# Reading a matmul's moving operand as two interleaved halves, in a fused attention and two feed-forward layers on one core

## The chip, the core and the metric

The kernel runs on one core of a Trainium2 chip. A core has a matrix engine (TensorE, PE in the rows below, with PEld for its weight loads), a vector engine (VectorE, DVE), a scalar engine (ScalarE, ACT), GpSimd (POOL) and a sync engine (SP) that issues most transfers. The metric is the device time of one execution in microseconds (us); lower is better. All arithmetic on the device counts, and the arrangement of inputs and outputs on the host doesn't.

A matmul on TensorE takes two operands from the on-chip memory SBUF. The stationary one (`lhsT`) is loaded first, as weights. The moving one (`rhs`) is then streamed through, column by column, and each of its columns gives one column of the result in the accumulation memory, PSUM.

## The reference

```
def _attn_ref(q, k, v, tau):                       # each 1 x 6016 x 256
    qn = q / (np.linalg.norm(q, axis=1, keepdims=True) + 1e-06)
    kn = k / (np.linalg.norm(k, axis=1, keepdims=True) + 1e-06)
    s = kn.transpose(0, 2, 1) @ qn / tau           # 256 x 256
    a = np.exp(s - s.max(-1, keepdims=True))
    a /= a.sum(-1, keepdims=True) + 1e-09
    return v @ a
x = attn.reshape(6016, 256)
h = x @ moe_w_in;  x = (h * np.clip(h + 3, 0, 6) / 6) @ moe_w_out     # 256 -> 2048 -> 256
h = x @ moe2_w_in; r = np.maximum(h, 0); out = (r * r) @ moe2_w_out   # 256 -> 2048 -> 256
```

All arrays are 32-bit floats; the weights of both layers arrive as 64-bit floats and are brought to 32 bits on the chip.

## The kernel before, in words

**Attention.** The 256 x 256 scores are summed over 47 tiles of 128 tokens (`score`, line 315), in plain float32. The softmax is applied to them, and the result `et` is multiplied into the first layer's input weights `wi1` (`m1_first`, `m1_whole`; tiles `mp`), so that the first layer can work on the tokens of `v` directly.

**The two layers.** The 6016 tokens are taken in 6 passes of two blocks each, of 512 columns (5 passes) or 448 columns (the last): `WIDTHS = [512] * 5 + [448]`. So there are 12 pairs of layer and pass, (j, p). Everything is laid out with features on the partitions and tokens in the columns, so that the tokens are always the moving operand. The only products whose moving operand isn't tokens are the 48 of tile `mp`, where it is a row of 512 columns of `wi1`. Each 32-bit operand is split into a high and a low part of type float32r (`split`), and a product of two such operands is three matmuls, high by high, low by high, high by low. `passes` (lines 332 to 339) issues these three in a row, and `low_last` (line 318 on) issues the same three with the low weight parts last.

From the second pair on, a layer's input product goes by a Strassen scheme (`strassen`): for each of 8 units of 256 hidden features, seven products (tiles `y`, `q`, `x`) take the place of eight. The output products (`group`, tile `acc`) are added up in four PSUM banks over the whole pass. The first pair (0, 0) has its own code: `first_products` (line 685), `whole_product` through `low_last` (line 327), and `second_both` (line 734).

Between an input product and its output product ScalarE and VectorE copy, add, gate and split the tile (`copy_out`, `add`, `relu`, `act`, `hi`, `lo`); line 132 is the subtraction that gives a low part. The order of all this is a list of events, each put at a place in a row of slots (`at`, `extra`, `run`), and every engine works through its own instructions in that order.

**What is streamed.** Each moving operand of these products is a stretch of one tile row, of 512 or 448 neighbouring columns. The result of a layer's last product goes through `evict` to `x2_d` in main memory (or to `out`), and is read back as the next layer's input. On the host, `kernel` lays out the tokens in `vt`, and the last lines put `out` back into the order of the reference.

Of the kernel before, what the change touches and what calls it, by code (L numbers as in the profile page):

```python
# [16 lines left out]
P = 128  # L17
C = 256
NTOK = 6016
DFF = 2048  # L20
NT = NTOK // P
KC = C // P
# [40 lines left out]
def attention_then_two_ffns(  # L63
# [44 lines left out]
    def bank(shape, name, tag=None):  # L108

        if tag is None:  # L110
            tag = "yxyq"[turn[0] % 4]
            turn[0] += 1
        return ps_h.tile(shape, F32, tag=tag, name=name, bufs=2 if tag == "y" else 1)
# [9 lines left out]

    def f32(x):
        return x.bitcast(F32)

    def split(hi, lo, x, part=2, eng=nc.vector):

        if part != 1:
            nc.scalar.copy(hi, x)  # L130
        if part != 0:
            eng.tensor_tensor(out=lo, in0=x, in1=f32(hi), op=ALU.subtract)  # L132
# [48 lines left out]
    wi1, wo1 = {}, {}  # L181
# [44 lines left out]
    def second_in(u):  # L226
# [25 lines left out]
        def rests(i):  # L252
            a, w = ((slice(0, S1), x[:, :S1, :]), (slice(S1, None), st))[i]
            nc.vector.tensor_tensor(out=lo[:, a, :], in0=w, in1=f32(hi[:, a, :]), op=ALU.subtract)

        def keep_out():
            for t, d in zip((hi, lo), wa2_d[u // 2]):
                nc.sync.dma_start(out=d[:, u % 2, :, :], in_=f32(t))
# [60 lines left out]
    def low_last(ps, pairs, weights=True, only=2):  # L319

        n = len(pairs)
        parts = ((0, 0), (0, 1)), ((1, 0),)
        for part in parts if only == 2 else parts[only:only + 1]:
            for i, (a, b) in enumerate(pairs):
                for x, y in part:
                    w, v = (a[x], b[y]) if weights else (b[y], a[x])
                    nc.tensor.matmul(  # L327
                        ps, lhsT=w, rhs=v, start=i == 0 and (x, y) == (0, 0), stop=i == n - 1 and x == 1
                    )

    def passes(ps, pairs, start=True, stop=True, more=False):


        n = len(pairs)
        for i, ((ah, al), (bh, bl)) in enumerate(pairs):
            first, last = start and i == 0, stop and i == n - 1
            nc.tensor.matmul(ps, lhsT=ah, rhs=bh, start=first, stop=False, skip_group_check=more)  # L337
            nc.tensor.matmul(ps, lhsT=al, rhs=bh, start=False, stop=False, skip_group_check=more)  # L338
            nc.tensor.matmul(ps, lhsT=ah, rhs=bl, start=False, stop=last, skip_group_check=more)  # L339

    with tc.manual_schedule():
# [9 lines left out]
        t = 0  # L351

        for gi, n in enumerate(GROUPS):
# [13 lines left out]
            for j in range(n):  # L367
                x = src[:, j * 2 * C:(j + 1) * 2 * C]
# [67 lines left out]
        x0 = {}  # L436
# [79 lines left out]
        def m1_first(i, part):  # L516
            if part != 1:
                mps[0, i] = bank([P, 512], f"mp0_{i}")
            low_last(mps[0, i], [
                ([t[:, i, j * P:(j + 1) * P] for t in et], [t[:, j, :] for t in wi1[0]]) for j in range(KC)  # L520
            ], only=part)

        def m1_whole(c4, i):
            mps[c4, i] = bank([P, 512], f"mp{c4}_{i}")
            low_last(mps[c4, i], [
                ([t[:, j, :] for t in wi1[c4]], [t[:, i, j * P:(j + 1) * P] for t in et]) for j in range(KC)
            ], False)
# [48 lines left out]
        def m1_sum(c4, i):  # L576

            if i == 0:
                m1_st[c4] = beside(max(c4, 1), 0).rearrange("p (u a c) -> p u a c", u=2, a=4)
            m = [m32[c4][:, k, :].rearrange("p (u f c) -> p u f c", u=2, f=2) for k in range(KC)]  # L580
            combine(i, m1_st[c4], [[t[:, :, f, :] for f in range(2)] for t in m], lambda t, i: t[:, :, i, :], idle_first(c4 < 2))

        def m1_sums_split(c4, u, part):
            hi, lo = (t[:, u, S1:, :] for t in wa1[c4])
            split(hi, lo, m1_st[c4][:, u, :, :], part, idle_first(c4 < 2))
# [30 lines left out]
        acc = {}  # L616
# [5 lines left out]
        def group(j, p, u, f, n, d, gs, first, last):  # L622

            w = WIDTHS[p]
            if first:
                acc[j, p, n, d] = ps_acc.tile([P, WMAX], F32, tag="acc", name=f"acc{j}_{p}_{n}_{d}")[:, :w]
            wo = wo_parts(j, u)
            at = f * C + d * P
            passes(acc[j, p, n, d], [([wo[:, i, at:at + P] for i in range(2)], gs)], first, last)
# [36 lines left out]
        hs = {}  # L666
# [3 lines left out]
        def weight0(f, k):  # L670
            c4, u, odd = f // 4, f // 2 % 2, f % 2
            if odd and k == 0:
                return [a21[c4][:, i, u, :] for i in range(2)]
            return [t[:, u, (A12, A22)[odd] if k else A11, :] for t in wa1[c4]]

        def first_products():
            for at in range(2):
                n, f = steps[at]
                hs[at] = bank([P, WMAX], f"h0_{n}_{f}")[:, :w0]
            for k in range(KC):  # L680
                for part in ((0, 0), (0, 1)), ((1, 0),):
                    for at in range(2):
                        n, f = steps[at]
                        for a, b in part:
                            nc.tensor.matmul(
                                hs[at], lhsT=weight0(f, k)[a], rhs=x0[k, n][b],
                                start=k == 0 and (a, b) == (0, 0), stop=k == KC - 1 and a == 1,
                            )

        def whole_product(at):  # L690
            if at < len(steps):
                n, f = steps[at]
                name = f"h0_{n}_{f}"
                if at in (2, 3):
                    hs[at] = ps_acc.tile([P, WMAX], F32, tag="acc", name=name)[:, :w0]
                else:
                    hs[at] = bank([P, WMAX], name)[:, :w0]
                low_last(hs[at], [(weight0(f, k), x0[k, n]) for k in range(KC)])
# [27 lines left out]
        def second_both(n, f, gs):  # L726
            u, at = f // 2, f % 2 * C
            if f == 0:
                for d in range(KC):
                    acc[0, 0, n, d] = ps_acc.tile([P, WMAX], F32, tag="acc", name=f"acc0_0_{n}_{d}")[:, :w0]  # L730
            for part in ((0, 0), (1, 0)), ((0, 1),):
                for d in range(KC):
                    for i, k in part:
                        nc.tensor.matmul(  # L734
                            acc[0, 0, n, d], lhsT=wo1[u][:, i, at + d * P:at + (d + 1) * P], rhs=gs[k],
                            start=f == 0 and (i, k) == (0, 0), stop=f == KF - 1 and k == 1,
                        )

        def drain(limit):
            while len(pending) > limit:  # L740
                second_both(*pending.pop(0))
# [24 lines left out]
        def extra(place, go):  # L766


            while any(abs(place - x) < (APART if place > 0 else APART_FIRST) for x in taken):
                place += 0.3  # L770
            taken.append(place)
            at(place, go)
            return place
# [61 lines left out]
        def strassen(j, p, u, at0):  # L835
# [7 lines left out]
            def mult(r):  # L843
                wa = wa1[c4] if j == 0 else wa2[c4]
                if r == B11:
                    s["y"] = bank([P, WMAX], f"y{name}", "y")[:, :w]
                elif r == B21:
                    s["x"] = bank([P, WMAX], f"x{name}", "x")[:, :w]
                elif r == T3:
                    s["q"] = bank([P, WMAX], f"q{name}", "q")[:, :w]  # L850
                to = {B21: "x", T3: "q", T4: "q"}.get(r, "y")
                passes(
                    s[to], [([t[:, ui, WEIGHT[r], :] for t in wa], operands[j, p, r])],
                    r in (B11, B21, T3), more=r not in (B11, B21, T3),
                )
# [66 lines left out]
        k = 0  # L922
# [11 lines left out]
        for c4, x in ((0, -100), (1, -72), (2, 10), (3, 34)):  # L934
            for i in range(4):
                x = extra(x, lambda c4=c4, i=i: m1_sum(c4, i)) + 1
            for u in range(2):
                at(x + 2 + u, lambda c4=c4, u=u: m1_sums_split(c4, u, 0))
            for u in range(2):
                x = extra(x + 4 - 3 * u, lambda c4=c4, u=u: m1_sums_split(c4, u, 1))  # L940
# [49 lines left out]
        def four_steps():  # L990
# [44 lines left out]
            run(-(len(steps) - 4) * SLOTS / 4)  # L1035

        first_products()
        relu0(0)
        four_steps()
        for a, (n, f) in enumerate(steps):  # L1040
            if a < 4:
                continue
            part, since = divmod(a + M1_LEAD, 8)
# [36 lines left out]
        for x, go in zip(LEFT_AT, [(n, f, d, gs) for n, f, gs in pending for d in range(KC)], strict=True):  # L1080
            n, f, d, gs = go
# [48 lines left out]
```

## Time and profile before

| | |
|---|---|
| Time of one execution, median of 3 runs | 1036.01 us (1035.68 to 1036.33) |
| Span of the profiled execution, first to last instruction | 1033.6 us |
| Left of the median outside that span | 2.4 us |
| TensorE busy | 1027.0 us, 99% of the span |
| TensorE weight loads busy | 866.0 us, 84% |
| VectorE busy | 849.0 us, 82% |
| ScalarE busy | 664.8 us, 64% |
| GpSimd busy | 42.6 us, 4% |

The profile is of one execution, for which the span is given and no time of its own besides; the median stands 2.4 us above it. Busy time is the union of an engine's instructions. A matmul's record is longer than the time until the next one starts, because matmuls overlap in the engine; the pace of TensorE is therefore read from the start times of its matmuls, not from their durations.

### The profile page before, as it was taken

The numbers are of one execution on the slowest core, as the hardware profiler recorded it, in microseconds if no ns is written. First come the engines' busy times: TensorE is split into PE (matmuls) and PEld (weight loads), VectorE is DVE, ScalarE is ACT, GpSimd is POOL, SyncE is SP. The second block draws the span as 40 slices with busy tenths as digits, with TensorE's granted clock in tenths as the row PEclk, the third lists the DMA queues.
The fourth block names the chain that finished last, engine by engine and source line by source line (L and its number), as shares of the span: only waits on it lengthen the run. The fifth ranks groups of instructions, "written<-read, shape, count | busy, mean of one in ns | idle before, by whom it ended". The sixth has DMA issues, their size and how long they took to land.

```text
span 1033.6 us, 12918 instructions
## 1 busy us (share of the span) xinstructions
PE 1027.0 (99%) x4618; PEld 866.0 (84%) x4618; DVE 849.0 (82%) x1419; ACT 664.8 (64%) x1202; POOL 42.6 (4%) x42
## 2 busy tenths in 40 slices
PE   9999999999999999999999999999999999999998
PEld 8888888888888888888998888888888888888997
DVE  5899988889989989889988688688778688778765
ACT  7788877778787778878775445455445455445543
POOL 2212330000000000000000000000000000000000
PEclk9999999999999999999999999999999999999999
DMA  9811212003403403403745002002002000100100
GB/s 360 345 58 42 81 47 96 1 1 139 137 1 123 152 1 118 153 1 131 263 160 185 1 1 82 0 1 82 1 1 75 7 1 25 52 1 1 41 1 36
DMA packets 26368, 77.64 MB, mean 75 GB/s; under 512 B 2880, under 2 KB 5056, under 8 KB 26304
## 3 DMA queue, kind: packets, MB, share of 16 engines
q1 hardware_dynamic: 26160, 76.70, 20.9%
q8 instruction: 36, 0.59, 0.2%
q14 instruction: 28, 0.23, 0.1%
q10 hardware_dynamic: 144, 0.11, 0.0%
HBM read 52.95 MB, written 23.86 MB: 74 GB/s over the span
## 4 chain that ended last, share of the span: by engine, by line
PE 99%; DVE 0%; ACT 0%; issue 0%; POOL 0%; POOLq 0%
PE acc L339 15%; PE acc L338 15%; PE acc L337 15%; PE y L338 8%; PE y L337 8%; PE y L339 8%; PE s L315 4%; PE h L327 4%; PE acc L734 4%; PE q L337 4%; PE q L339 4%; PE q L338 4%; PE x L339 2%; PE x L337 2%; PE x L338 2%; PE mp L327 1%
## 5 line engine op out<-in xcount | busy, mean ns | idle before, releaser
L132 DVE TENSOR_TENSOR gs<-g,gs 128x512 fp32r<-128x512 f32 (+1 forms) x384 | 263.5, 687 | 58.8 <-ACT gs L886 48.2
L339 PE MATMUL acc<-gs,wo 128*128 128x512 f32 (+1 forms) x708 | 272.6, 385 | 0.1
L338 PE MATMUL acc<-gs,wo 128*128 128x512 f32 (+1 forms) x708 | 272.5, 385 | 0.0
L337 PE MATMUL acc<-gs,wo 128*128 128x512 f32 (+1 forms) x708 | 272.4, 385 | 0.0
L886 ACT CAST gs<-g 128x512 fp32r<-128x512 f32 (+1 forms) x352 | 208.0, 612 | 27.8 <-DVE g L877 19.0
L339 PEld LDWEIGHTS acc<-gs,wo 128*128 128x128 f32 x708 | 132.9, 188 | 25.3 <-DVE gs L132 0.5
L338 PEld LDWEIGHTS acc<-gs,wo 128*128 128x128 f32 x708 | 132.9, 188 | 24.3
L337 PEld LDWEIGHTS acc<-gs,wo 128*128 128x128 f32 x708 | 132.9, 188 | 24.3
L859 ACT COPY se<-y 128x512 f32<-128x512 f32 (+1 forms) x88 | 50.7, 576 | 123.4 <-PE y L339 123.3
L863 DVE TENSOR_TENSOR h<-q,se 128x512 f32<-128x512 f32 (+1 forms) x88 | 59.6, 677 | 64.9 <-ACT se L859 64.4
L859 ACT COPY su<-y 128x512 f32<-128x512 f32 (+1 forms) x88 | 50.8, 577 | 87.1 <-PE y L339 76.2
L882 DVE SCALAR_TENSOR_TENSOR g<-h 128x512 f32<-128x512 f32 (+1 forms) x144 | 97.0, 674 | 0.0
L869 ACT ACTIVATE r<-h,three 128x512 f32<-128x512 f32 (+1 forms) x120 | 85.5, 713 | 8.0 <-DVE h L863 7.7
L877 DVE SCALAR_TENSOR_TENSOR g<-r,h 128x512 f32<-128x512 f32 (+1 forms) x120 | 80.8, 673 | 3.9 <-ACT r L869 3.8
L871 ACT ACTIVATE r<-y 128x512 f32<-128x512 f32 (+1 forms) x48 | 28.3, 589 | 62.8 <-PE y L339 62.8
L863 DVE TENSOR_TENSOR h<-q,su 128x512 f32<-128x512 f32 (+1 forms) x88 | 59.5, 676 | 1.5
L863 DVE TENSOR_TENSOR h<-x,sa 128x512 f32<-128x512 f32 (+1 forms) x88 | 59.2, 673 | 0.0
L859 ACT COPY sa<-y 128x512 f32<-128x512 f32 (+1 forms) x88 | 50.7, 576 | 7.3 <-PE y L339 1.3
L882 DVE SCALAR_TENSOR_TENSOR g<-y,r 128x512 f32<-128x512 f32 (+1 forms) x48 | 32.7, 681 | 23.6 <-ACT r L871 23.0
L734 PE MATMUL acc<-gs,wo 128*128 128x512 f32 x180 | 45.0, 389 | 0.0
L315 PE MATMUL s<-qk 128*128 128x256 f32 x188 | 42.1, 385 | 0.0
L315 PEld LDWEIGHTS s<-qk 128*128 128x128 f32 x188 | 36.1, 194 | 5.1 <-DMA qk<-in_qk 0.2
(245 smaller groups left out, 1803.3 us busy)
## 6 DMA issues: line engine op xcount, KB each, us to landing
qk<-in_qk SPq DMA_DIRECT2D x21, 512.0 KB, 10.0
wo<-in_w_out SPq DMA_DIRECT2D x16, 512.0 KB, 5.6
wi<-in_w_in SPq DMA_DIRECT2D x10, 512.0 KB, 5.5
x2d<-o SPq DMA_DIRECT2D x20, 256.0 KB, 2.5
raw<-x2d SPq DMA_DIRECT2D x10, 512.0 KB, 5.5
out<-o SPq DMA_DIRECT2D x20, 256.0 KB, 2.3
raw<-in_vt SPq DMA_DIRECT2D x8, 512.0 KB, 5.8
wo2d<-wo2s SPq DMA_DIRECT2D x8, 512.0 KB, 2.9
```

Source lines behind the costliest of these rows:

```text
L132: eng.tensor_tensor(out=lo, in0=x, in1=f32(hi), op=ALU.subtract)
L315: nc.tensor.matmul(s_ps[i], lhsT=x[:, C + i * P:C + (i + 1) * P], rhs=x[:, :C], start=(t == 0), stop=(t == NT - 1))
L337: nc.tensor.matmul(ps, lhsT=ah, rhs=bh, start=first, stop=False, skip_group_check=more)
L338: nc.tensor.matmul(ps, lhsT=al, rhs=bh, start=False, stop=False, skip_group_check=more)
L339: nc.tensor.matmul(ps, lhsT=ah, rhs=bl, start=False, stop=last, skip_group_check=more)
L734: nc.tensor.matmul(acc[0, 0, n, d], lhsT=wo1[u][:, i, at + d * P:at + (d + 1) * P], rhs=gs[k], start=f == 0 and (i, k) == (0, 0), stop=f = ...
L859: nc.scalar.copy(s[tag], s["y"])
L863: nc.vector.tensor_tensor(out=s[which], in0=s[ps], in1=s[tag], op=ALU.add)
L869: nc.scalar.activation(s["r" + which], h, AF.Relu, bias=three)
L877: nc.vector.scalar_tensor_tensor(out=g, in0=s["r" + which], scalar=6.0, in1=h, op0=ALU.min, op1=ALU.mult)
L882: nc.vector.scalar_tensor_tensor(out=g, in0=h, scalar=0.0, in1=r, op0=ALU.max, op1=ALU.mult)
L886: nc.scalar.copy(gs[which][0], s["g" + which])
```

## The change

A new helper `halves` views a row of w columns as w/2 pairs: the first column of the first half, the first of the second half, the second of the first half, and so on. In the layers' matmuls the moving operand is now this view. The tile in SBUF is the same, and so are its place and its size; only the order in which its columns are streamed differs. Neighbours in that order lie 256 columns apart (224 in the last pass), which is 1024 or 896 bytes of each partition's row, and column c of the result holds another token than before.

Four such products follow on each other for every token (into and out of each layer), so the tokens come out permuted four times over. The last lines of `kernel` compute that permutation and undo it on the host. Where the moving operand is a row of `wi1`, the columns of the weights are laid out on the host so that the product comes out in the old order (`interleaved`). The score product and the small ones of the softmax keep their plain rows.

```
+    def halves(x):
+
+        return x.rearrange("p (a b) -> p b a", a=2)
...
# low_last
-                        ps, lhsT=w, rhs=v, start=i == 0 and (x, y) == (0, 0), stop=i == n - 1 and x == 1
+                        ps, lhsT=w, rhs=halves(v), start=i == 0 and (x, y) == (0, 0), stop=i == n - 1 and x == 1
...
# passes
             first, last = start and i == 0, stop and i == n - 1
+            bh, bl = halves(bh), halves(bl)
             nc.tensor.matmul(ps, lhsT=ah, rhs=bh, start=first, stop=False, skip_group_check=more)
...
# first_products
-                                hs[at], lhsT=weight0(f, k)[a], rhs=x0[k, n][b],
+                                hs[at], lhsT=weight0(f, k)[a], rhs=halves(x0[k, n][b]),
...
# second_both
-                            acc[0, 0, n, d], lhsT=wo1[u][:, i, at + d * P:at + (d + 1) * P], rhs=gs[k],
+                            acc[0, 0, n, d], lhsT=wo1[u][:, i, at + d * P:at + (d + 1) * P], rhs=halves(gs[k]),
...
# kernel, on the host
+    def interleaved(w):
+        return w.reshape(KC * P, DFF // 512, 256, 2).transpose(0, 1, 3, 2).reshape(KC * P, DFF)
...
-        "w_in1": w_in(inputs["moe_w_in"]),
+        "w_in1": w_in(interleaved(inputs["moe_w_in"])),
...
-        res[t:t + 2 * w] = got[p, :, :, :, :w].transpose(2, 3, 1, 0).reshape(2 * w, KC, P)
+        at = np.arange(w)
+        for _ in range(4):
+            at = at.reshape(2, w // 2).T.reshape(w)
+        part = np.empty((P, KC, 2, w), got.dtype)
+        part[..., at] = got[p, :, :, :, :w]
+        res[t:t + 2 * w] = part.transpose(2, 3, 1, 0).reshape(2 * w, KC, P)
```

Every engine has the same instructions in the same order in both kernels; only an operand of each of these matmuls reads otherwise.

## Rows read from the trace of the kernel before

**Rows 1.** The page's chain of work that ended last, by engine.
```profile
PE 99%; DVE 0%; ACT 0%; issue 0%; POOL 0%; POOLq 0%
```
**Rows 2.** Waits of PE: who waited for whom, us in total, times, longest.
```profile
PE busy L294 <- POOL both L119: 1.1, 1, 1.1
PE mp L327 <- ACT eth L502: 0.5, 1, 0.5
```
**Rows 3.** Windows: stretch, PE, PEld, DVE, ACT, POOL busy (instructions), granted clock, DMA.
```profile
0.00:49.00 49.00, 47.41 (x225) 41.74 (x225) 34.23 (x64) 37.04 (x68) 13.18 (x19) 1.00 0.94 370
49.00:1028.80 979.80, 979.60 (x4394) 824.23 (x4394) 814.39 (x1355) 627.48 (x1134) 29.38 (x23) 1.00 0.17 60
1028.80:1033.60 4.80, 0.00 (x0) 0.00 (x0) 0.39 (x1) 0.30 (x1) 0.00 (x0) 0.99 0.52 191
```
**Rows 4.** Windows over the whole span, PE of one line alone: L337, L734, L327, L685.
```profile
0.00:1033.60 1033.60, 509.37 (x1324) 1.00 0.21 75
```
```profile
0.00:1033.60 1033.60, 45.02 (x180) 1.00 0.21 75
```
```profile
0.00:1033.60 1033.60, 56.76 (x228) 1.00 0.21 75
```
```profile
0.00:1033.60 1033.60, 2.88 (x12) 1.00 0.21 75
```
**Rows 5.** Groups of L338 with 448 columns, shapes kept apart, one for each tile.
```profile
L338 PE MATMUL acc<-gs,wo 128*128 128x448 f32 x128 | 46.8, 366 | 0.0
...
L338 PE MATMUL y<-x,wa_0l 128*128 128x448 f32 x16 | 5.9, 368 | 0.0
...
L338 PE MATMUL q<-x,wa_0l 128*128 128x448 f32 x8 | 2.9, 364 | 0.0
...
L338 PE MATMUL x<-x,wa_0l 128*128 128x448 f32 x4 | 1.4, 362 | 0.0
```
**Rows 6.** Timeline of PE, 600 to 606 us: start, us, what. First and last of 28.
```profile
599.70 0.39 PE L338 MATMUL acc<-gs,wo 128*128 128x512 f32 x1
599.93 0.39 PE L339 MATMUL acc<-gs,wo 128*128 128x512 f32 x1
...
605.82 0.39 PE L338 MATMUL y<-x,wa_3l 128*128 128x512 f32 x1
```
**Rows 7.** Timeline of PE, 968 to 972 us. First and last of 21.
```profile
967.77 0.36 PE L339 MATMUL y<-x,wa_0h 128*128 128x448 f32 x1
967.97 0.36 PE L337 MATMUL y<-x,wa_1h 128*128 128x448 f32 x1
...
971.82 0.36 PE L338 MATMUL acc<-gs,wo 128*128 128x448 f32 x1
```
**Rows 8.** Timeline of PE, 25 to 43 us, like instructions merged: start, us, what.
```profile
24.66 17.00 PE L315 MATMUL s<-qk 128*128 128x256 f32 x78
41.49 1.73 PE L409 MATMUL nrm<-both,scratch 128*128 128x1 f32 x15
```
**Rows 9.** Instructions of L315 and L409: duration ns min/median/max, first and last start.
```profile
L315 PE MATMUL s<-qk x188: 379/379/634, 4.3 to 47.9; 128*128 128x256 f32 x188
```
```profile
L409 PE MATMUL nrm<-both,scratch x16: 167/250/250, 41.5 to 43.1; 128*128 128x1 f32 x16
```
**Rows 10.** Windows as in 3, of the stretch with the densest work beside PE.
```profile
160.00:600.00 440.00, 440.00 (x1980) 371.32 (x1979) 385.27 (x664) 327.72 (x589) 0.00 (x0) 1.00 0.27 94
```

## The prediction

> **What bounds the kernel now.** I read the chain of waits first. TensorE holds 99% of the chain that ended last [rows 1], and its own list of waits is two entries long, 1.6 us together [rows 2]. So nothing feeds TensorE late; the time is the number of its matmuls times their pace. The window table then says where the changed matmuls lie: all in the 979.8 us from 49.0 to 1028.8 us, in which TensorE is busy for 979.6 us at a granted clock of 1.00, which is the 2.4 GHz level [rows 3]. Ahead of it lies the score stage, and behind it 4.8 us of eviction and output; neither is touched.
>
> The counts come from the lines. Line 337 issues 1324 matmuls, and 338 and 339, the other two of the same three, as many; 734 issues 180, 327 issues 228 and 685 issues 12 [rows 4]. That is 3 x 1324 + 420 = 4392. Those with 448 columns are, for each of lines 337 to 339, 128 for `acc`, 16 for each of four groups of `y`, 8 for each of four of `q`, 4 for each of four of `x` [rows 5]: 128 + 4 x 28 = 240, so 720 in all. The other 3672 have 512 columns.
>
> The pace comes from start times. In the timeline of a steady stretch 27 starts lie between 599.70 and 605.82 us: 226.7 ns for a matmul of 512 columns [rows 6]. With 448 columns 20 of them take from 967.77 to 971.82 us: 202.5 ns [rows 7]. The check: 3672 x 0.2267 + 720 x 0.2025 = 832.4 + 145.8 = 978.2 us of the 979.6 in the window.
>
> **What one column costs.** At 2.4 GHz 512 columns at one per clock would be 213.3 ns, and 448 would be 186.7. The layers' matmuls are 13.4 and 15.8 ns above that. The score product, plain float32, shows another pace: 78 matmuls of 256 columns take 17.00 us, the last of them 0.38 [rows 8, 9], so each takes (17.00 - 0.38) / 77 = 215.8 ns, two clocks per column and only 2.5 ns over. And 15 matmuls of one column each, whose pace is that of loading 128 columns of weights, take (1.73 - 0.25) / 14 = 106 ns [rows 8, 9], 0.83 ns per weight column.
>
> Side by side: wherever else this trace shows TensorE taking 4-byte elements from SBUF, it takes one per 0.83 to 0.84 ns (score stream, weights). Only the layers' plain rows come at one per 0.443 ns, nearly two per such beat, and they alone miss the clock by 6%. I read this as a supply of columns that runs at its limit, and that gets there because two neighbours arrive together. That is an argument, not a row; the score product also has two clocks of arithmetic per column, so its pace may be the array's and not the memory's.
>
> **The change, part by part.** No instruction is added, removed or moved, on any engine or queue, and no wait. The transfers have the same sizes and shapes. The host's new orders cost nothing on the chip. Evictions, gates and splits work on plain rows as before. What is left is one thing: 4392 matmuls stream their 512 or 448 columns so that each column lies 1024 or 896 bytes from the one before. Nothing hides a change of pace there, since TensorE has no idle time to give; each ns per matmul is 4392 x 1 ns = 4.4 us.
>
> The trace has no moving operand read in such an order, so I bound its price. From below: the best pace that a row shows for 512 clocks of streaming is the score product's 215.8 ns [rows 8], a gain of 10.9 ns, and 188.8 ns for 448 columns, a gain of 13.7. From above: if no two columns come together any more, each costs what one costs alone. By the score stream that is 0.843 ns per column, 431.6 ns for 512 and 377.7 for 448. If instead the pace of today is halved outright, it is 453.4 and 405.0 ns.
>
> I take the upper end, at the score product's price. The plain rows already miss the clock at 0.443 ns per column, so the supply has no slack in which a worse order could hide, and the new order takes away the one thing that sets these reads apart from the two slower kinds: that what is wanted next lies beside what was just read.
>
> The sum: 3672 x (431.6 - 226.7) ns = 752.4 us, and 720 x (377.7 - 202.5) = 126.1 us, together +878.5. From the profiled span: 1033.6 + 878.5 = 1912.1, and with the 2.4 us by which the median stands above the span, **1914.5 us**. At exactly one column per 1.2 GHz beat (426.7 and 373.3 ns) it is +857 and 1893 us; at double today's pace +978 and 2014 us. VectorE's 849 us and ScalarE's 665 us of work [rows 3] don't grow and fall under half of the span, so neither can become the bound.
>
> [...]
>
> **The rivals.**
>
> *Faster: the 10.9 ns go away.* The place is the stream of each layers' matmul. That two kinds of matmul stream for 512 clocks, one 2.5 ns over the clock and the other 13.4, shows that the excess isn't the engine's own cost for a matmul. If it comes from reading along a row (always drawing on the part of the memory that is already busy), alternating between two places could spare it. Price: 3672 x 10.9 + 720 x 13.7 ns = 40.0 + 9.9 = 49.9 us, 986 us. It decides from 0.5 ns per matmul on (2.1 us, 0.2%). Against it: the excess is there in every tile and buffer alike, and nothing says that distance helps rather than hurts. Beside TensorE, VectorE has 385.3 us of work in 440 [rows 10]; shortened by 5% that stretch would be 419 us, which still holds it, though some of the gain could become waits.
>
> *No change: the order doesn't matter.* If the column supply fetches element by element and its limit is in the count of bytes, any order costs 226.7 ns. The time stays 1036 us. For it: the stream's addresses are known ahead. Against it: the two slower kinds of read above. [...]
>
> *Slower, but far from double.* The excess is paid per jump in address order and merely grows. Doubled, it is 3672 x 13.4 + 720 x 15.8 ns = 60.6 us, 1097 us; between there and 1893 any multiple is possible. For it: an excess exists that a mere break could enlarge. Against it: it needs a supply that mostly manages single columns at 0.44 ns, of which no row speaks.
>
> **How the numbers follow.** I give the full price, one column at a time, 0.40; the smaller slowdown 0.12; no change 0.14; the gain 0.34, rather high for what the rows support, because the excess of 13.4 ns is real and the order of reading is one of the few things that could be behind it. Differences under 0.2% (2 us) can't be told from no change by such runs, so: faster 0.34, same 0.14, slower 0.52. The likeliest case is 1914 us, with a range of its own of 1890 to 2016. To hold the time 8 times in 10 the range has to take in both the gain and the full price, since leaving out either leaves out more than 2 in 10: 984 to 2016 us. It is wide because the one price that decides isn't in the trace and multiplies 4392 times.
>
> **What would show it right or wrong.** In the timeline of the changed kernel the starts of 512-column matmuls in a steady stretch should lie 427 to 454 ns apart, those of 448 columns 373 to 405, alike in `acc`, `y`, `q`, `x`; the score product should keep 215.8 ns. TensorE should stay at 99% of the chain and at a granted clock of 1.00, and VectorE should show long idle times that TensorE ends. If the starts lie 216 ns apart, the supply is helped by distance; if they lie at 226.7, the order is free; and if TensorE shows waits, something else moved that I have not seen.

## The result, and the profile after

The changed kernel takes 996.39 us (median of 4 runs, 996.07 to 996.87) against 1036.17 us before: ratio 0.9615, 95% interval 0.9601 to 0.9629. It is faster by 39.8 us, where 1914 us was forecast.

The page of the kernel after, its head and the first lines of its chain that ended last:

```profile
span 995.1 us, 12918 instructions
...
PE 983.1 (99%) x4618; PEld 869.0 (87%) x4618; DVE 845.0 (85%) x1419; ACT 676.5 (68%) x1202; POOL 42.0 (4%) x42
...
PE 84%; DVE 7%; ACT 4%; DMA 2%; issue 2%; SPq 1%; ACTq 0%; DVEq 0%
```

The same instructions, and TensorE is still busy for 99%. But the chain, 99% TensorE before [rows 1], now goes through VectorE and ScalarE for 11%. The pace is in the timeline of TensorE, 600 to 606 us, first and last of 30 rows (start, us, what), and 935 to 939 us, first and last of 23:

```profile
599.69 0.38 PE L343 MATMUL q<-x,wa_3l 128*128 128x512 f32 x1
599.91 0.38 PE L344 MATMUL q<-x,wa_3h 128*128 128x512 f32 x1
...
605.95 0.38 PE L342 MATMUL x<-x,wa_0h 128*128 128x512 f32 x1
```

```profile
934.71 0.35 PE L344 MATMUL x<-x,wa_1h 128*128 128x448 f32 x1
934.90 0.35 PE L342 MATMUL acc<-gs,wo 128*128 128x448 f32 x1
...
938.88 0.35 PE L342 MATMUL y<-x,wa_1h 128*128 128x448 f32 x1
```

29 starts in 6.26 us are 215.9 ns for 512 columns (226.7 in [rows 6]), and 22 in 4.17 us are 189.5 ns for 448 (202.5 in [rows 7]). Over the whole trace nearly every start-to-start time is 215 or 216 and 189 or 190 ns, in all tiles alike, 215.8 and 189.2 on the mean without the waits. These two differ by 26.6 ns for 64 columns, which gives an estimate of 0.416 ns a column. That is 2.4 GHz if a column takes one clock, the frequency that the prediction counts with; [rows 3] show a granted clock of 1.00 and no frequency. 512 and 448 such clocks are 213.3 and 186.7 ns, and both paces lie 2.5 ns above them. The excess of the plain rows, 13.4 and 15.8 ns, is down to that. The windows show what the pace did not give (columns as in [rows 3]):

```profile
49.00:990.00 941.00, 935.34 (x4394) 827.33 (x4394) 811.49 (x1358) 638.93 (x1134) 28.84 (x23) 1.00 0.18 62
```

At the new pace 4392 matmuls are 3672 x 0.2158 + 720 x 0.1892 = 928.6 us; the stretch is 941.0. Some 12 us of it are waits and what follows them, against under 2 before. TensorE's list of waits, two entries long before [rows 2], reads now, in part:

```profile
PE acc L739 <- DVE gs L136: 1.5, 2, 0.8
...
PE h L331 <- DVE g L716: 1.0, 2, 0.5
PE acc L344 <- DVE gs L136: 0.7, 3, 0.3
PE acc L739 <- DVE wo L136: 0.6, 1, 0.6
PE h L331 <- DVE wa_1l L557: 0.6, 1, 0.6
```

One of them in the timeline, 72 to 76.5 us:

```profile
75.13 0.48 PE L331 MATMUL h<-x,wa_1l 128*128 128x512 f32 x1
76.17 0.48 PE L331 MATMUL h<-x,wa_1l 128*128 128x512 f32 x1 [0.57 <-DVE wa_1l L557]
76.49 0.38 PE L331 MATMUL h<-x,wa_1h 128*128 128x512 f32 x1
```

The start at 76.17 comes 1.04 us after the last one instead of 0.22, and the next one needs 0.32 us: the list's 0.57 us is a loss of 0.93. Added up from the start times, between 50 and 150 us 7.5 us are lost in this way, and later 4.2.

### The profile page after: what moved, and what is told of

Same layout as the page of the kernel before. It is cut to its first block, busy times and chain, and to the rows that moved or that the text cites. A ratio compares the mean times of both kernels' runs of the same rounds, so it can differ in the third digit from the quotient of the medians.

```text
span 995.1 us, 12918 instructions
## 1 busy us (share of the span) xinstructions
PE 983.1 (99%) x4618; PEld 869.0 (87%) x4618; DVE 845.0 (85%) x1419; ACT 676.5 (68%) x1202; POOL 42.0 (4%) x42
## 4 chain that ended last, share of the span: by engine, by line
PE 84%; DVE 7%; ACT 4%; DMA 2%; issue 2%; SPq 1%; ACTq 0%; DVEq 0%
PE acc L344 14%; PE acc L342 14%; PE acc L343 14%; PE y L342 7%; PE y L344 7%; PE y L343 7%; PE q L342 4%; PE q L344 4%; PE q L343 4%; PE s L319 4%; DVE gs L136 2%; PE x L342 2%; PE x L344 2%; PE x L343 2%; ACT gs L134 1%
## 5 line engine op out<-in xcount | busy, mean ns | idle before, releaser
L344 PE MATMUL acc<-gs,wo 128*128 128x512 f32 (+1 forms) x708 | 265.9, 376 | 0.8 <-DVE gs L136 0.7
L342 PE MATMUL acc<-gs,wo 128*128 128x512 f32 (+1 forms) x708 | 264.9, 374 | 0.0
L343 PE MATMUL acc<-gs,wo 128*128 128x512 f32 (+1 forms) x708 | 264.9, 374 | 0.0
L344 PEld LDWEIGHTS acc<-gs,wo 128*128 128x128 f32 x708 | 133.8, 189 | 19.5 <-DVE gs L136 3.6
L343 PEld LDWEIGHTS acc<-gs,wo 128*128 128x128 f32 x708 | 133.8, 189 | 15.5
L342 PEld LDWEIGHTS acc<-gs,wo 128*128 128x128 f32 x708 | 133.8, 189 | 15.5
L739 PEld LDWEIGHTS acc<-gs,wo 128*128 128x128 f32 x180 | 33.5, 189 | 8.6 <-DVE gs L136 2.6
```

The lines of the kernel that those rows point to most:

```text
L739: nc.tensor.matmul(acc[0, 0, n, d], lhsT=wo1[u][:, i, at + d * P:at + (d + 1) * P], rhs=halves(gs[k]), start=f == 0 and (i, k) == (0, 0), ...
```

## The experiments

**1. Form, number of streams, and the weight load.** Three theories were on the table for the excess of the plain row: it is paid where stream and weight load meet (meeting), it is the stream's own and distance spares it (row), or the operand's form counts (form).

```
plain_pairs   halves(x) = x.rearrange("p (b a) -> p b a", a=2)
quarters      halves(x) = x.rearrange("p (a b) -> p b a", a=4)
w2_plain      kernel before; lhsT=wo[:, i, f * C + d:(f + 1) * C:2]      # acc, was at:at + P
w2_halves     kernel after;  the same
```

> The layers' moving operand is viewed as pairs of neighbours, (0, 1), (2, 3), and so on: the three-dimensional form of the change with the order of before. Three theories for the excess of 10.9 ns per 512-column matmul. Meeting: the stream (one column per clock) runs through the rows twice as fast as the next weight load (one per two clocks), and the excess is paid where they meet; two halves run at the weights' speed and never meet them. Row: the excess belongs to the stream alone, which is too fast for one place, and is spared by alternating between distant ones. Form: an operand with two free dimensions starts sooner, whatever the order. Meeting and row expect 226.7 ns and about 1036 us here, form 215.8 ns and about 996 us.

> Four interleaved quarters in place of two halves (the host's orders follow). Row and form expect what halves gave, 215.8 ns and about 996 us, since neighbours in the order are still far apart. Meeting expects part of the excess back: each place is now passed through at half the weights' speed, so the load overtakes the stream, half as often as the stream overtook the load before; some 5 ns of the 10.9, about 221 ns and 1015 us.

> The kernel before, with its plain rows, but the output products (tile acc, 2304 of the 4392 matmuls) load every second column of 256 as weights in place of 128 neighbours, so that the load runs through the row as fast as the stream does (the host orders the output weights to match). Meeting expects 215.8 ns in acc and still 226.7 ns in y, q and x, about 1010 us. Row and form expect 226.7 ns everywhere and about 1036 us, since the stream is unchanged.

> The changed kernel with the same weights at every second column in the output products. Meeting expects the excess back in acc, where the load now runs twice as fast as the interleaved stream: some 5 to 11 ns, about 1010 to 1022 us. Row and form expect 215.8 ns everywhere and about 996 us.

Measured, one execution each: `plain_pairs` 1036.07 us at 226.7 ns, but its trace shows an operand with one dimension of 512, so the form was merged away and the run tells nothing of it. That form alone gains nothing shows in `near8` below, whose operand keeps three dimensions (2, 2, 128) and stays at 226.7 ns. `quarters` 1249.5 us, slower by a fifth, which no theory had expected. `w2_plain` 1051.6 us: acc rose to 233.2 ns instead of falling. `w2_halves` 996.5 us: 215.8 ns as with neighbouring weights. The meeting theory fell on both sides, and the row and form theories by the quarters, where both had expected 215.8 ns. Timeline of `quarters`, 700 to 706 us, first and last of 22 rows (21 starts in 5.95 us, 283 ns; 278 on the mean of the whole trace):

```profile
699.81 0.45 PE L343 MATMUL y<-x,wa_2l 128*128 128x512 f32 x1
...
705.76 0.45 PE L343 MATMUL x<-x,wa_2l 128*128 128x512 f32 x1
```

**2. Distance and step.** The host's orders follow each view of the moving operand, in these runs and in those that come after, so that the tokens come out in place.

```
near512    x.rearrange("p (c a b) -> p c b a", c=2, a=2)
near16     x.rearrange("p (c a b) -> p c b a", a=2, b=4)
even_odd   x.rearrange("p (a b) -> p b a", b=2)
step4      x.rearrange("p (a b) -> p b a", b=4)
```

> Two interleaved streams as in the change, but half as far apart: each half of the row is itself read as two interleaved quarters, 512 bytes apart (448 in the last pass). Quarters gave 278 ns, so either the distance of 512 bytes is bad or four streams are too many. Two theories. Count: the column supply keeps two places of a row at hand and refetches with more; two streams at any distance give 215.8 ns and about 996 us. Distance: streams must be 1024 bytes apart; here 278 ns as with quarters, about 1250 us.

> Two interleaved streams only 16 bytes apart: in each group of eight columns the order is 0, 4, 1, 5, 2, 6, 3, 7. Count expects 215.8 ns and about 996 us if the places are 16 bytes long, since again two are in use, each for four columns. Distance expects no gain: 226.7 ns as in a plain row (about 1036 us) or worse.

> The even columns of a row, then the odd ones: a single stream with a step of 8 bytes, each place passed through twice as fast. Count, with places of 16 bytes of which a stretch of two columns is used, expects more fetches per column than a plain row and so more than 226.7 ns; 230 to 280 ns, 1050 to 1260 us. Distance, in which the excess comes of neighbours lying side by side, expects about 226.7 ns or less, since neighbours in the order are still near.

> Every fourth column, four times over: a single stream with a step of 16 bytes, so that no two columns in a row share 16 bytes. Count expects a fetch for each column, as with quarters: about 278 ns, 1250 us; if a fetch takes two clocks, 427 ns and 1890 us. If a column alone cost no more than one beside its neighbour, 226.7 ns.

Measured: `near512` 997.2 and `near16` 992.75 us, both at 215.8 ns, so two streams do at 16 bytes what they do at 1024, and distance isn't the point. Timeline of `near16`, 700 to 706 us, first and last of 29 rows (28 starts in 6.05 us):

```profile
699.80 0.38 PE L343 MATMUL acc<-gs,wo 128*128 128x512 f32 x1
...
705.85 0.38 PE L344 MATMUL acc<-gs,wo 128*128 128x512 f32 x1
```

`even_odd` took 1997.0 us at 451 ns, where 230 to 280 was expected; `step4` 2041.4 us at 461 ns. The price that the prediction had put on the interleaved halves (431.6 ns, or 453.4 at double the pace of before) exists, but it belongs to a step of 8 bytes from one column to the next. Timeline of `even_odd`, 1200 to 1206 us, first and last of 15 rows (14 starts in 6.31 us):

```profile
1199.67 0.63 PE L344 MATMUL acc<-gs,wo 128*128 128x512 f32 x1
...
1205.98 0.63 PE L343 MATMUL y<-x,wa_0l 128*128 128x512 f32 x1
```

A step of two columns doubles the time of a matmul (451 ns), and two streams 16 bytes apart don't (215.8). What can set the two apart is the step from a column to the next but one in the stream: 16 bytes in `even_odd`, mostly 4 in `near16`; in a plain row it is 8, in the halves 4. The expectations that come next put this as a theory of two readers. It is the author's guess, and no trace shows readers; what the runs can show is whether the pace follows that step.

**3. The step to the next but one, and again the weight load.**

```
near8         x.rearrange("p (c a b) -> p c b a", a=2, b=2)
halves_even   x.rearrange("p (a b c) -> p c b a", a=2, c=2)
w0_plain      kernel before; lhsT=wo[:, i, f * C + d:f * C + d + 1].to_broadcast([P, P])
w4_plain      kernel before; lhsT=wo[:, i, 2 * f + d::4]
```

> In each group of four columns the order is 0, 2, 1, 3: two interleaved streams 8 bytes apart, so that columns taken in turn lie in the same 16 bytes as in a plain row. Two theories for what halves do. Two readers: the stream is served by two readers in turns, each at one column per two clocks; a reader is free of stalls if it stays for four columns in the same 16 bytes (halves, 16 bytes apart) and saturated if it stays for two (plain row); here each stays for two, so about 226.7 ns and 1036 us. Pairs: what counts is that the place of a column is used again two columns later rather than at once; 215.8 ns and about 994 us.

> Two interleaved halves, each read by its even columns first and then by its odd ones: neighbours in the order are 1024 bytes apart, and each of the two streams steps by 8 bytes. Two readers expects each reader to stay for two columns in 16 bytes, as in a plain row: about 226.7 ns and 1036 us, against 451 ns for the single stream with a step of 8 bytes. Pairs of neighbours fetched together (a fetch brings 8 bytes, each used for one column here) expects 451 ns and about 2000 us as in the single stream.

> The kernel before with plain rows, but each output product (tile acc) loads one column of the output weights 128 times over (step 0) in place of 128 neighbours, so that the load needs next to nothing of the memory; this leaves out all but one of 128 columns of the output weights of both layers. Two theories. Steal: a plain row uses every turn of the memory that TensorE's stream has, and the weight load takes turns from it, one clock for each 16 bytes (32 for 128 neighbours); here acc falls to about 215.8 ns, near 1010 us. Stream alone: the excess has nothing to do with what the load reads, 226.7 ns and 1036 us.

> The kernel before with plain rows, but each output product loads every fourth of 512 columns as weights, a new 16 bytes for each (the host orders the output weights to match). With every second column acc was 233.2 ns, 17.4 above 215.8, where neighbours cost 10.9. Steal expects more again: 128 stretches of 16 bytes in place of 64 and 32, so some 25 to 55 ns over 215.8, 1070 to 1130 us. Stream alone expects 226.7 to 233 ns.

Measured: `near8` 1036.1 us and `halves_even` 1034.5 us, both at 226.7 ns, as two readers expects, and not the 215.8 or 451 ns of the theories beside it. Timelines of TensorE, 700 to 706 us, first and last of 28 rows, of `near8` and of `halves_even` (27 starts in 6.12 us each):

```profile
699.71 0.39 PE L343 MATMUL q<-x,wa_3l 128*128 128x512 f32 x1
...
705.83 0.39 PE L343 MATMUL q<-x,wa_3l 128*128 128x512 f32 x1
```

```profile
699.67 0.39 PE L343 MATMUL acc<-gs,wo 128*128 128x512 f32 x1
...
705.79 0.39 PE L343 MATMUL x<-x,wa_0l 128*128 128x512 f32 x1
```

`w0_plain` took 1045.0 us, with acc at 231.3 ns where the load reads a single column; `w4_plain` 1069.0 us, with acc at 233.6 ns (512 columns). So to load one column over and over doesn't bring acc down to 215.8 ns, and the theory that the load takes turns away from the stream fell too; but 231.3 isn't the 226.7 ns of stream alone either.

The 33 us of `w4_plain` are more than 7 ns on 1920 matmuls of acc can give (13 us). Its acc takes 233 to 234 ns with 448 columns as well, where a plain row takes 202.5, and the record of its weight load has grown from 188 ns in the kernel before to 311. The group of loads in `w4_plain`, and the first and last of four starts between 1030 and 1031.1 us (0.70 us for three):

```profile
L337 PEld LDWEIGHTS acc<-gs,wo 128*128 128x128 f32 x708 | 219.9, 311 | 14.2
```

```profile
1030.39 0.40 PE L337 MATMUL acc<-gs,wo 128*128 128x448 f32 x1
...
1031.09 0.36 PE L337 MATMUL q<-x,wa_2h 128*128 128x448 f32 x1
```

That the pace no longer depends on the columns fits a load that has itself become the limit, so this run says little of the stream. Its y and q of 512 columns, whose loads are unchanged, rose too, to 232 ns, which stays unexplained. Apart from it, what a load reads moves a 512-column plain row by up to 6.5 ns, always upward from 226.7 (231.3 in `w0_plain`, 233.2 in `w2_plain`).

**4. The stream by itself.** The kernel before with groups of matmuls after its end:

```
+        def measure(name, v, w, n=48):
+            ps = bank([P, 512], name)
...
+                nc.tensor.matmul(ps[:cols, :size], lhsT=w, rhs=v, start=True, stop=True)
+        row, lot = wo_of[NU - 1][:, 0, :], wa2[3][0][:, 0, 0, :]
+        measure("plain_quarter", row, lot[:, :32])
+        measure("short_halves", f32(row)[:, :256].rearrange("p (a b) -> p b a", a=2), f32(lot))
...
```

> The kernel before, with 16 groups of 48 matmuls after its end on fixed operands, whose results are not used. Per matmul of 512 columns, with 128 columns of weights: plain 226.7 ns, halves and streams 32 bytes apart 215.8, quarters 278, evens 451, fours 461, if nothing else on the chip has a part in it. With 64 and 32 columns of weights a plain row stays at 226.7 ns if the excess is the stream's own, and falls by about 5 and 8 ns if it is the load's. The plain float32 products (256 columns, two clocks each) take 215.8 ns in a row. Two readers that take columns in turns expect them, if both clocks of a column count as a turn of one reader, to stay at 215.8 ns with interleaved halves and with a step of 8 bytes, since a new 16 bytes is needed every four clocks at the most; a memory that charges for the step itself expects about twice that.

The timeline of TensorE merges each group into a row (start, us, what); the time until the next row's start, over the count, is the pace:

```profile
1029.81 11.07 PE L1092 MATMUL plain_all<-wo,wa_3h 128*128 128x512 f32 x48
1040.71 11.20 PE L1092 MATMUL plain_half<-wo,wa_3h 128*64 128x512 f32 x48
1051.75 11.29 PE L1092 MATMUL plain_quarter<-wo,wa_3h 128*32 128x512 f32 x48
1062.87 10.52 PE L1092 MATMUL halves_all<-wo,wa_3h 128*128 128x512 f32 x48
...
1083.59 13.76 PE L1092 MATMUL quarters_all<-wo,wa_3h 128*128 128x512 f32 x48
...
1110.61 23.58 PE L1092 MATMUL eighths_all<-wo,wa_3h 128*128 128x512 f32 x48
1134.01 21.84 PE L1092 MATMUL evens_all<-wo,wa_3h 128*128 128x512 f32 x48
...
1199.45 10.54 PE L1092 MATMUL near_all<-wo,wa_3h 128*128 128x512 f32 x48
1209.83 20.88 PE L1092 MATMUL short_all<-wo,wa_3h 128*128 128x256 f32 x96
1230.55 26.40 PE L1092 MATMUL short_halves<-wo,wa_3h 128*128 128x256 f32 x96
1256.78 21.92 PE L1092 MATMUL short_evens<-wo,wa_3h 128*128 128x256 f32 x96
1278.54 21.92 PE L1092 MATMUL short_fours<-wo,wa_3h 128*128 128x128 f32 x96
```

A plain row keeps its excess with 64 and 32 columns of weights (230.0 and 231.7 ns, and 227.1 with 128, from the start times), and with no other engine at work: the excess is the stream's own. The float32 groups went against what was written down, that they stay at 215.8 ns: interleaved halves give 273.3 ns, a step of 8 bytes 226.7, and a step of 16 bytes 226.7 for half as many columns. But these are figures of the float32r streams again. A float32 stream, at 0.843 ns a column in a row, goes by the step from a column to the next as a float32r stream goes by the step to the next but one:

| the step: in float32r to the next column but one, in float32 to the next | float32r order: ns per 512 | float32 order: ns per 256 |
|---|---|---|
| 4 bytes | halves, 512, 64, 32 and 16 bytes apart: 215.8 | plain row: 215.8 |
| 8 bytes | plain row, near8, halves_even: 226.7 | step of 8 bytes: 226.7 |
| 16 bytes | even_odd: 451 | step of 16 bytes: 453 (2 x 226.7 for 128) |
| to and fro between two places | quarters: 278 to 283 | halves: 273.3 |

The first three rows follow the step. From 8 bytes to 16 the time doubles (226.7 to 451 ns for float32r, 226.7 to 453 for float32), and at 32 bytes, in `step4`, it is hardly more (461 ns). By the same proportion a step of 4 bytes would come to some 113 ns, an estimate from the 226.7; that is less than the 213.3 ns of a column per clock, which the measured 215.8 ns are 2.5 above. Read so, the plain row's 226.7 ns are the price of its step, and not the stream's time with something added. This was worked out afterwards from the paces, and no run was built to test it.

**5. Where 10 us went, and the best order.**

```
near16_pool   near16, and in unit(): split(..., eng=nc.gpsimd) from the fourth piece on
near16_lag3   near16, LAG = 3, and drain(LAG if a < len(steps) - 1 else 2)
near64        x.rearrange("p (c a b) -> p c b a", a=2, b=16)
```

> The streams 16 bytes apart again, timed. One look gave 992.75 us, against 996.4 us for halves, at the same pace of 215.8 ns in both. If the 3.6 us are the luck of one execution, about 996 us; if the order that is written and read has a part in VectorE's and ScalarE's stalls, 993 us.

> The same, and the low parts of the first layer's weights that are converted beside the first pair (11 of its 14 pieces) are subtracted on GpSimd instead of VectorE. If the missing 10 us are VectorE being late for TensorE, most of the waits between 50 and 150 us go away (4.7 us in near16, 7.5 us in halves): 988 to 990 us. If they come from elsewhere, or GpSimd holds VectorE up in turn, 993 us or more.

> The streams 16 bytes apart, and in the first pair's stage the output products follow three steps behind the input products instead of two. If TensorE waits there because it asks for a gated and split tile too early, the waits on those tiles go and some 1 to 3 us with them: 990 to 992 us. If VectorE and ScalarE are late as a whole, or if the waits are those on the folded weights, which this doesn't touch, 993 us.

> The changed kernel once more, on the same chip as the run beside it. If the 3.3 us by which streams 16 bytes apart are ahead are a matter of that one chip, about 993 us; if they belong to the order, 996 us.

> Two interleaved streams 64 bytes apart. Two readers expects 215.8 ns again. If ScalarE's reads with a step of 8 bytes are held up by streams that lie far apart, they stay at 665 to 670 ns here, and the time is near 993 us; if any distance beyond 16 bytes holds them up, 840 to 870 ns, and 996 us.

`near16_timed`: 993.05 us, ratio 0.9585 (0.9571 to 0.9599). `halves_again`: 996.69 us, 0.9620 (0.9604 to 0.9636), on another chip (the kernel before took 1036.0 us on the one and 1035.8 on the other). The two intervals don't meet, so the order 0, 4, 1, 5, 2, 6, 3, 7 is ahead of the changed kernel by 3.6 us and of the kernel before by 43; streams 64 bytes apart do as well in the one execution that was measured (`near64`: 992.8 us). The difference lies in waits and late starts of TensorE: by its start times `near16_timed` loses 4.4 us between 50 and 150 us and 2.9 later, where the changed kernel loses 7.5 and 4.2. Part of the cause is visible on ScalarE, which reads the raw weights with a step of 8 bytes. Its group `tbwo` (mean ns behind the comma) in the kernel before, after, near512, near16_timed, near64 and halves_even:

```profile
L161 ACT ACTIVATE tbwo<-wo 128x512 f32<-128x512 f32 x16 | 10.7, 670 | 0.0
```

```profile
L165 ACT ACTIVATE tbwo<-wo 128x512 f32<-128x512 f32 x16 | 13.7, 858 | 0.0
```

```profile
L165 ACT ACTIVATE tbwo<-wo 128x512 f32<-128x512 f32 x16 | 13.8, 860 | 0.0
```

```profile
L165 ACT ACTIVATE tbwo<-wo 128x512 f32<-128x512 f32 x16 | 10.7, 671 | 0.0
```

```profile
L165 ACT ACTIVATE tbwo<-wo 128x512 f32<-128x512 f32 x16 | 10.9, 682 | 0.0
```

```profile
L165 ACT ACTIVATE tbwo<-wo 128x512 f32<-128x512 f32 x16 | 10.8, 672 | 0.0
```

These reads take longer beside halves and streams 512 bytes apart, and hardly longer beside streams 16 and 64 bytes apart. Distance alone isn't the reason: the streams of `halves_even` lie 1024 bytes apart too, and the reads stay at 672 ns beside them. What they and the stream meet in stays open, and that this is the whole of the 3.6 us isn't shown. `near16_pool` took 993.62 us (0.9592) and `near16_lag3` 993.95 us (0.9595): neither is better than `near16`. Less work for VectorE moved the waits to GpSimd's and ScalarE's results, in TensorE's list of waits of `near16_pool`:

```profile
PE mp L331 <- POOL wi1l L136: 0.9, 2, 0.7
PE acc L740 <- ACT gs L134: 0.7, 1, 0.7
```

That fits a stage of the first pair that is late as a whole at the new pace; which of its engines would have to be relieved first stays open.

## Why the prediction was wrong, point by point

**What bounds the kernel** held: the pace of TensorE's matmuls decided, and it changed on all 4392 alike, as the counts said. The likeliest case, 1914 us, was wrong in its direction; the wide range of 984 to 2016 us took in the measured 996.4 us only because it reached down to the rival "faster".

**The step that failed** is the price: "if no two columns come together any more, each costs what one costs alone", with the upper end of the bounds taken from it. The two rows behind it were rightly read, and that the plain row runs at a limit of its supply fits the paces (at twice its step the time doubles, from 226.7 to 451 ns). But the conclusion, that it is fast because neighbours in the stream arrive together, was turned around. The halves, with no two neighbours together, take 215.8 ns and not 431.6. From a column to the next but one the plain row has a step of 8 bytes and takes 226.7 ns, 10.9 more than the halves, where that step is 4. Why every second column should count is not shown, and the two readers of the expectations are a guess at it. The guess foretold `near8` and `halves_even` and failed on the float32 groups as first put; the step, as put in the table, sorts every pace there, with a price of its own for `quarters` and the float32 halves (to and fro between two places) that was measured and not foretold. The doubled pace is real, but it belongs to a step of 16 bytes or more to the next but one (`even_odd` 451 ns, `step4` 461).

**The rival "faster"** had the right row for its bound, 215.8 ns, and nearly the right pace for 448 columns (188.8 forecast, 189.2 measured), but a wrong reason: alternating between two places isn't what spares the excess, since `halves_even` alternates between places 1024 bytes apart and stays at 226.7 ns, and `near8` between places 8 bytes apart. Its 986 us was off by 10 us for the reason that it named as a risk, work beside TensorE that doesn't shrink. The risk was looked for in the dense stretch from 160 to 600 us, though; of the 12 us of waits and late starts 7.5 lie between 50 and 150 us.

**"No change" and "slower, but far from double"** didn't come about; a slowdown of the second kind exists with four streams (1250 us).

**Still open:** why the plain row's excess is larger for 448 columns (15.8 ns) than for 512 (13.4); it is 13 ns in `halves_even`, where the step to the next but one is the same (and the time, 1034.5 us, 1.4 us under that of the kernel before on its chip). Why the pace goes by every second column. What in a weight load raises a plain row's time by up to 7 ns (233.2 and 233.6 against 226.7). And why two places in turn cost 278 to 283 ns (273.3 in float32), less than the 451 ns of a step of 16 bytes.

## What to carry to other kernels

When TensorE is the bound, set the start-to-start time of its matmuls against the time of their columns (0.416 ns each here): an excess that is the same in every tile (6% here) can be a matter of how the operand is read, and here it was had back by the order of the columns alone. For float32r streams try an order in which each column lies beside the last but one, four such columns at a time (0, 4, 1, 5, 2, 6, 3, 7, in `near16`, took 215.8 ns instead of 226.7; 0, 2, 1, 3, in `near8`, gained nothing), and let the layout of inputs and outputs take up the permutation. For plain float32 the row as it is was the fastest (215.8 ns for 256 columns; 226.7 with a step of 8 bytes, 273.3 in halves). After such a gain look for the stage where the other engines had no slack left: here it gave back a fifth of it (10 us of a forecast 50).

## What the runs showed of the hardware that was not expected

- A float32r moving operand costs 226.7 ns per 512 columns in a row and 215.8 in two interleaved streams of neighbours, 16, 32, 512 or 1024 bytes apart (64 by its time, 992.8 us); a step of 8 bytes from one column to the next doubles it (451 ns), four streams cost 278 to 283 and eight 487 ns.
- For plain float32 it is the other way round: in a row 215.8 ns per 256 columns, in interleaved halves 273.3.
- ScalarE's reads with a step of 8 bytes rise from 670 to 858 ns beside the halves, and stay at 671 to 682 ns beside streams 16 and 64 bytes apart and in `halves_even`.
- Weights read from every fourth column (`w4_plain`) make the load's record 311 ns instead of 188, and hold a matmul to 233 ns whether it has 512 columns or 448.
- The first matmul after a wait holds the next one back too: 0.32 us from start to start instead of 0.216, in the timeline of the result and after the other waits of that trace (0.29 instead of 0.189 with 448 columns).
